# Attention and mixture of experts on one core: the softmax sums leave in two transfers instead of four

## The chip, the core and the metric

The kernel runs on one core of a Trainium2 chip. TensorE does the matmuls, VectorE and ScalarE work on tiles, GpSimd on tiles in SBUF, and the sync engine (SP) issues nearly all transfers. The metric is device time in microseconds, the median of several runs.

## The reference, cut to what matters

```python
q_rot, k_rot = (rotate(q), rotate(k))                 # batch 8, 8 heads, 576 positions, 64 wide
scores = scale * np.matmul(q_rot, k_rot.transpose(0, 1, 3, 2))
attn = np.exp(scores - np.max(scores, axis=-1, keepdims=True))
attn = attn / (np.sum(attn, axis=-1, keepdims=True) + 1e-09)
x = np.matmul(attn, v)                                # heads side by side: (4608, 512)
...
logits = x @ phi                                      # 32 slots, 4 for each of 8 experts
slot_input = softmax(logits, over tokens).T @ x
slot_out[e] = np.maximum(slot_input[e] @ w1[e], 0.0) @ w2[e]
return softmax(logits, over slots) @ slot_out
```

The change touches one thing: how the row sums of `exp(scores)` become factors 1/sum that are multiplied into the attention output.

## The kernel before, in words

Two heads make a pair; there are 32 pairs, four to a batch. A pair takes some 12.7 to 16 us, and the work of several pairs overlaps. The tables `WHEN`, `EARLY` and `ENDS` give each task of each pair a time, and the program is written out in the order of these times. So every engine, SP among them, has its instructions in a fixed order and waits in line at each.

The tasks of a pair, in the order in which they follow from each other: `load0` and `load1` fetch q and k (`x_in`, L171), `spin0` and `spin1` multiply by cosine and sine on GpSimd (L176), `join` adds on VectorE (L180), `high` and `low` split the result in two half-precision tiles (`hl`, L185 on ScalarE and L189 on VectorE). `m_unit` (L209, L211) makes the scores in one precision and takes their row maxima on VectorE; these go through `m_turn`, `m_half` and the two small transfers of `m_rows` (L239, L240) into a tile `peak`. `t_unit` (L257) makes the scores again, with the maxima subtracted by a matmul on `peak`, and ScalarE takes exp (L258). `av` (L273) multiplies by v. 

Then the sums, for the first 30 pairs. VectorE adds weight tables (`add1`, L287, and `add2`, L291). `total` (L304) sums over keys with matmuls by the selector `pick`; the sums lie in four blocks of 32 partitions (two halves n of the 576 positions, two partial sums k), and of each block two partitions count, one for each head. `total_out` (L309) copies them to `s4` on ScalarE. `send` (L315) re-cuts them by transfers from SBUF to SBUF: 2 partitions of 288 numbers become 48 partitions of `RC` = 12 numbers, four transfers in all. `recip` (L321, L322) adds the two partial sums and takes 1/x on VectorE. `spread` (L328) writes the result to a row in device memory (`r_row`), `widen` (L335) reads it back, repeated over 64 partitions for each head (`rb`), and `norm` (L339) multiplies on GpSimd. `logits` (L429) needs that product later.

On SP the order in a pair is: `x_in` (load0), a weight tile `w_exp`, `v_in`, the transfers of `send`, the two of `m_rows`, `x_in` (load1), `spread`, two of `widen`. Each transfer also waits for the one issued eight places ahead of it, because eight semaphores (DMAHW0 to DMAHW7) are given out in turn. On VectorE `recip` stands between `add1` and `add2`, and `low` comes right after.

The last two pairs take another way (`sums_rows`, `sums_turn`), which uses `pick` too. After the pairs come the experts: weights w1 and w2 stream in, and the output is written.

Of the kernel before, what the change touches and what calls it, by code (L numbers as in the profile page):

```python
# [7 lines left out]
F32 = mybir.dt.float32  # L8
# [3 lines left out]
ALU = mybir.AluOpType  # L12
AX = mybir.AxisListType
# [8 lines left out]
NS = E * SPE  # L22
# [4 lines left out]
HC = S // 2  # L27
# [16 lines left out]
N_HEAT = 16  # L44
N_CST = 2
FILL = (3, 1, 1, 2, 2, 5)
RC = 12
PIECE = 4
WHEN = {
# [40 lines left out]
def attn_softmoe(ctx, tc, qk, v, phi, w1, w2, cs, ident, sel, seg, out):  # L90
    nc = tc.nc
    P = 128

    const = ctx.enter_context(tc.tile_pool(name="const", bufs=1))
    small = ctx.enter_context(tc.tile_pool(name="small", bufs=3))
# [22 lines left out]
    rows = (slice(0, 64), slice(64, P))  # L118
# [11 lines left out]
    peaks = [const.tile([P, S], F16, name=f"peak{i}") for i in range(2)]  # L130
    for t in peaks:
        nc.vector.memset(t, 0.0)
    pick = const.tile([P, NS + 1], F32, name="pick")
    nc.gpsimd.memset(pick, 0.0)
    for h in (0, 1, 2):
        nc.gpsimd.memset(pick[rows[h % 2], h:h + 1], 1.0)

    nc.vector.memset(tiny, 0.0)
    for n in range(2):
        nc.vector.memset(tiny[64 * n:64 * n + 32], 1e-9)  # L140
    l_sb = const.tile([P, 2, 193], F32, name="l_sb")
    nc.vector.memset(l_sb[:, 0, 192:193], -BIG)
    d_t = const.tile([P, P], F32, name="d_t")
# [147 lines left out]
        nc.vector.tensor_tensor(out=c, in0=c, in1=weights_of(p, 4), op=ALU.add)  # L291

    sg = {}
    rcs = [const.tile([48, 2, 2, RC], F32, name=f"rc{i}") for i in range(2)]

    def total(p):
        c = cts.pop(p)
        sg[p] = s = bank2()[:, 0, 0:HC]
        for i in range(3):
            for n in range(2):  # L300
                for k in range(2):
                    at = 32 * (2 * n + k)
                    rhs = weights_of(p, 3 + 2 * i + k) if i else c[:, k]
                    nc.tensor.matmul(s[at:at + 32], lhsT=pick[:, n:n + NS], rhs=rhs[:, half[n]],  # L304
                                     start=(i == 0), stop=(i == 2), tile_position=(0, at))

    def total_out(p):
# [3 lines left out]

    def send(p, eng):
        s4, rc = sg.pop(p), rcs[p % 2]
        for i in range(4):
            eng.dma_start(out=rc[:, i // 2, i % 2, :], in_=s4[32 * i:32 * i + 2])  # L315

    rbs = {}

    def recip(p):
        rr = small.tile([48, 2, RC], F32, name="rr", bufs=2)  # L320
        nc.vector.tensor_reduce(out=rr, in_=rcs[p % 2].rearrange("p n k x -> p n x k"), axis=AX.X, op=ALU.add)  # L321
        nc.vector.reciprocal(out=rr, in_=rr)  # L322
        sg[p] = rr

    def spread(p, eng):
        rr = sg.pop(p)
        rd = dram.tile([2, 2, HC], F32, name="r_row")
        eng.dma_start(out=rd.rearrange("n h (r x) -> (h r) n x", x=RC), in_=rr)  # L328
        sg[p] = rd

    def widen(p, eng):
# [32 lines left out]
    def sums_rows(p):  # L364
        z = cts.pop(p)[:, 0]
        t = flat.pop("h") if "h" in flat else bank2()
        for i in range(4):
            nc.tensor.matmul(t[32 * i:32 * i + 32, 0, 0:HC], lhsT=pick[:, i % 2:i % 2 + NS], rhs=z[:, half[i % 2]],
                             start=True, stop=True, tile_position=(0, 32 * i))
        sg[p] = s4 = late.tile([P, HC], F32, name="s4", bufs=1)  # L370
        nc.vector.tensor_copy(out=s4, in_=t[:, 0, 0:HC])

    def sums_turn(p, t=None):
        s4, t = sg.pop(p), bank2() if t is None else t
        rn = small.tile([P, 3, 2, 2], F32, name="rn", bufs=2)
        for j, c in enumerate(turns):
            nc.tensor.transpose(t[:, 0, P * j:P * j + P], s4[:, c:c + P], id_sb)
        v = t[:, 0, 0:3 * P].rearrange("p (j n r) -> p j n r", j=3, r=32)
        nc.vector.reciprocal(out=rn, in_=v[:, :, 0:2, 0:2])
        sg[p] = rn  # L380

    def sums_wide(p, t=None):
# [344 lines left out]
    p = NPAIR - 1  # L727
# [8 lines left out]
    t = bank2()  # L736
# [288 lines left out]
```

## Time and profile before

| | |
|---|---|
| three runs | 566.99, 568.9, 570.32 us; median 568.9 |
| the profiled execution | 567.57 us, of which the span shown is 565.8 us |
| TensorE busy | 523.2 us, 92% of the span |
| VectorE, ScalarE, GpSimd busy | 77%, 57%, 52% |
| share of the 16 transfer engines | 60.2% for the kernel's own queue |

The shares are means over stages: a start of some 45 us, a long even stretch of pairs to about 500 us, and the experts. What an engine waited for is read in the stretch. Times are us from the start of the span; an engine's idle time is put down to what ended it.

### The profile page before, as it was taken

What the parts mean: (1) busy time and instruction counts of PE and PEld (TensorE: products, weight loads), DVE (VectorE), ACT (ScalarE), POOL (GpSimd) and SP (SyncE); (2) the same over time, 40 slices, a digit from 0 to 9 for tenths busy, and PEclk for the clock granted to TensorE, in tenths of its full rate; (3) what the DMA queues carried; (4) which work ended last, traced back from release to release, by engine and by line L of the source; (5) the groups of instructions that cost most, each with busy time, mean ns of one, the idle gap of its engine ahead of it and who ended that gap; (6) DMA issues with size and microseconds to landing.
All of it is one profiled execution on the core that took longest, in us unless ns stands there. A gap on an engine that the chain in (4) does not pass through costs nothing.

```text
span 565.8 us, 23624 instructions
## 1 busy us (share of the span) xinstructions
PE 523.2 (92%) x10302; PEld 351.2 (62%) x10302; DVE 435.9 (77%) x644; ACT 325.2 (57%) x639; POOL 296.0 (52%) x331
## 2 busy tenths in 40 slices
PE   4599999999989999999999999998999999999991
PEld 2266666666766676676666666666767665744551
DVE  5898989888888898788888888988888955642252
ACT  2156656666656565766676566665766665326641
POOL 2958666667656585865674848666656111011100
PEclk9599999999999999999999999999999999999997
DMA  7434555555564555555555556546635245999999
GB/s 261 153 105 166 188 187 187 187 187 185 161 203 157 189 187 187 188 187 185 185 192 173 197 144 222 174 134 197 196 125 186 76 134 163 308 346 346 331 304 293
DMA packets 69815, 111.38 MB, mean 197 GB/s; under 512 B 14416, under 2 KB 49488, under 8 KB 69712
## 3 DMA queue, kind: packets, MB, share of 16 engines
q1 hardware_dynamic: 69698, 109.87, 60.2%
q8 instruction: 81, 1.33, 1.0%
q14 instruction: 22, 0.18, 0.1%
q10 hardware_dynamic: 14, 0.00, 0.0%
HBM read 99.93 MB, written 9.58 MB: 194 GB/s over the span
## 4 chain that ended last, share of the span: by engine, by line
PE 62%; DVE 13%; DMA 10%; ACT 5%; SPq 4%; issue 4%; POOL 2%; DVEq 0%; ACTq 0%; POOLq 0%
PE o_ps L273 16%; PE s_ps L257 16%; PE s_ps L304 7%; PE s_ps L209 5%; DMA x_in<-in_qk 4%; DVE nm L211 3%; DVE hl L189 3%; DMA rc<-s 3%; PE s_ps L400 3%; SPq L315 3%; PE s_ps L866 2%; DMA rb<-r_row 2%; DVE c_t L291 2%; PE t_ps L918 2%; PE s_ps L429 2%
## 5 line engine op out<-in xcount | busy, mean ns | idle before, releaser
L176 POOL TENSOR_TENSOR x_in<-x_in,cs_sb 128x288 f32<-128x288 f32 x248 | 227.9, 951 | 105.3 <-DMA x_in<-in_qk 103.4
L211 DVE TENSOR_REDUCE nm<-s_ps 128x2 f32<-128x576 f32 x256 | 182.9, 750 | 53.0 <-PE s_ps L209 52.2
L258 ACT ACTIVATE a_t<-s_ps 128x576 f32<-128x576 f32 x256 | 161.0, 649 | 83.8 <-PE s_ps L257 73.3
L257 PE MATMUL s_ps<-hl 64*64 64x288 f16 x3456 | 158.7, 285 | 5.2 <-ACT xn L414 4.6
L273 PE MATMUL o_ps<-a_t,v_in 64*64 64x288 f32 x2048 | 161.6, 405 | 0.7 <-ACT xt L281 0.3
L257 PEld LDWEIGHTS <-hl 64*64 64x64 f16 x3456 | 100.6, 106 | 42.0 <-issue 26.9
L209 PE MATMUL s_ps<-hl 64*64 64x288 f16 x1024 | 82.9, 294 | 9.8 <-DVE nm L211 9.1
L257 PE MATMUL s_ps<-peak,lift 64*64 64x288 f16 x1152 | 89.4, 283 | 0.7 <-DMA peak<-mr 0.7
L273 PEld LDWEIGHTS o_ps<-a_t,v_in 64*64 64x64 f32 x2048 | 71.8, 133 | 17.1 <-ACT xt L281 4.5
L339 POOL TENSOR_TENSOR xt<-xt,rb 128x576 f32<-128x576 f32 x29 | 45.4, 1564 | 70.0 <-DMA rb<-r_row 63.5
L209 PEld LDWEIGHTS <-hl 64*64 64x64 f16 x1024 | 42.4, 106 | 34.0 <-issue 19.3
L185 ACT CAST hl<-x_in 128x576 f16<-128x576 f32 (+1 forms) x66 | 42.7, 651 | 24.1 <-DVE x_in L180 24.1
L180 DVE TENSOR_TENSOR x_in<-x_in 128x1152 f32<-128x1152 f32 (+2 forms) x36 | 52.6, 1462 | 3.2 <-POOL x_in L176 2.7
L287 DVE TENSOR_TENSOR c_t<-a_t 128x1152 f32<-128x1152 f32 x32 | 49.3, 1541 | 0.0
L189 DVE TENSOR_TENSOR hl<-x_in,hl 128x1152 f16<-128x1152 f32 x32 | 44.4, 1387 | 0.9 <-ACT hl L185 0.9
L309 ACT ACTIVATE s<-s_ps,bits 128x288 f32<-128x288 f32 x30 | 15.0, 501 | 47.0 <-PE s_ps L304 25.9
L257 PEld LDWEIGHTS <-lift 64*64 64x64 f16 x1152 | 38.6, 107 | 1.9 <-issue 0.9
L304 PE MATMUL s_ps<-a_t,pick 128*32 128x288 f32 x360 | 34.4, 406 | 0.0
L281 ACT COPY xt<-o_ps 128x576 f32<-128x576 f32 x32 | 20.4, 638 | 17.1 <-PE o_ps L273 13.0
L219 DVE TENSOR_REDUCE nm<-s_ps 128x2 f32<-128x576 f32 x32 | 24.0, 751 | 1.5 <-PE s_ps L217 0.2
L304 PEld LDWEIGHTS s_ps<-a_t,pick 128*32 128x32 f32 x360 | 15.2, 110 | 13.5
L414 ACT COPY xn<-s_ps 128x512 f32<-128x512 f32 x31 | 16.8, 589 | 11.0 <-PE s_ps L400 10.9
(202 smaller groups left out, 566.1 us busy)
## 6 DMA issues: line engine op xcount, KB each, us to landing
x_in<-in_qk SPq DMA_DIRECT2D x62, 576.0 KB
w_exp<-in_w SPq DMA_DIRECT2D x57, 512.0 KB
v_in<-in_v SPq DMA_DIRECT2D x32, 576.0 KB
rb<-r_row SPq DMA_DIRECT2D x60, 144.0 KB
out<-w_exp SPq DMA_DIRECT2D x16, 512.0 KB
hl<-in_w SPq DMA_DIRECT2D x4, 512.0 KB
rc<-s SPq DMA_DIRECT2D x120, 2.2 KB
x_in<-in_qk SPq DMA_DIRECT2D x4, 288.0 KB
```

The source lines that it names most:

```text
L176: eng.tensor_tensor(out=x[:, :, c], in0=x[:, :, c], in1=cs_sb[:, :, c], op=ALU.mult)
L180: nc.vector.tensor_tensor(out=x[:, t, 0, c], in0=x[:, t, 0, c], in1=x[:, t, 1, c], op=ALU.add)
L185: nc.scalar.copy(out=halves[p][:, 1 + t, c], in_=loaded[p][:, t, 0, c])
L189: nc.vector.tensor_tensor(out=hl[:, 0:4:3], in0=x[:, :, 0], in1=hl[:, 1:3], op=ALU.subtract)
L209: nc.tensor.matmul(s[rows[c], h, 0:HC], lhsT=hl[rows[h], QH, at:at + D], rhs=hl[rows[h], KH, half[n]], start=True, stop=True)
L211: nc.vector.tensor_reduce(out=nms[p][:, n, j:8:4], in_=s[:, :, 0:HC], axis=AX.X, op=ALU.max, negate=True)
L257: nc.tensor.matmul(s[rows[h ^ n], n, 0:HC], lhsT=lhs, rhs=rhs, start=(i == 0), stop=(i == 3))
L258: nc.scalar.activation(out=weights_of(p, b).rearrange("p (n x) -> p n x", n=2), in_=s[:, :, 0:HC], func=AF.Exp, scale=SCALE)
L273: nc.tensor.matmul(o[rows[h], n, 0:HC], lhsT=vt[r, b, n], rhs=a[r, half[n]], start=(b == 0), stop=(b == KB - 1))
L287: nc.vector.tensor_tensor(out=cts[p], in0=ats[p, 0], in1=ats[p, 1], op=ALU.add)
L304: nc.tensor.matmul(s[at:at + 32], lhsT=pick[:, n:n + NS], rhs=rhs[:, half[n]], start=(i == 0), stop=(i == 2), tile_position=(0, at))
L339: eng.tensor_tensor(out=xts[p], in0=xts[p], in1=rbs.pop(p), op=ALU.mult)
```

## The change

The two heads of a block come to lie 16 partitions apart instead of side by side (`pick` has its ones in columns 0, 16 and 32), and the blocks are put in the order k, then n. So the four rows of one partial sum lie at partitions 64k, 64k+16, 64k+32 and 64k+48, and one transfer with a step of 16 partitions takes them all. They are cut into 64 partitions of 18 numbers. `send` issues two transfers instead of four, `recip` works on 64 x 18 instead of 48 x 24 numbers, and `spread` writes 64 runs of 18 numbers instead of 96 of 12. No other task is moved. The small selector and the constant 1e-9 follow the new places, and `sums_turn` reads every 16th column.

```diff
--- before.py
+++ after.py
@@ -44,7 +44,8 @@
 N_HEAT = 16
 N_CST = 2
 FILL = (3, 1, 1, 2, 2, 5)
-RC = 12
+RC = 18
+HS = 16
 PIECE = 4
 WHEN = {
     "load0": -15.8683, "spin0": -15.5208, "load1": -12.695, "spin1": -12.6886, "join": -9.8416, "high0": -9.7692,
@@ -130,14 +131,13 @@
     peaks = [const.tile([P, S], F16, name=f"peak{i}") for i in range(2)]
     for t in peaks:
         nc.vector.memset(t, 0.0)
-    pick = const.tile([P, NS + 1], F32, name="pick")
+    pick = const.tile([P, NS + HS], F32, name="pick")
     nc.gpsimd.memset(pick, 0.0)
     for h in (0, 1, 2):
-        nc.gpsimd.memset(pick[rows[h % 2], h:h + 1], 1.0)
+        nc.gpsimd.memset(pick[rows[h % 2], HS * h:HS * h + 1], 1.0)
 
     nc.vector.memset(tiny, 0.0)
-    for n in range(2):
-        nc.vector.memset(tiny[64 * n:64 * n + 32], 1e-9)
+    nc.vector.memset(tiny[0:64], 1e-9)
     l_sb = const.tile([P, 2, 193], F32, name="l_sb")
     nc.vector.memset(l_sb[:, 0, 192:193], -BIG)
     d_t = const.tile([P, P], F32, name="d_t")
@@ -291,7 +291,7 @@
         nc.vector.tensor_tensor(out=c, in0=c, in1=weights_of(p, 4), op=ALU.add)
 
     sg = {}
-    rcs = [const.tile([48, 2, 2, RC], F32, name=f"rc{i}") for i in range(2)]
+    rcs = [const.tile([64, 2, RC], F32, name=f"rc{i}") for i in range(2)]
 
     def total(p):
         c = cts.pop(p)
@@ -299,9 +299,9 @@
         for i in range(3):
             for n in range(2):
                 for k in range(2):
-                    at = 32 * (2 * n + k)
+                    at = 32 * (2 * k + n)
                     rhs = weights_of(p, 3 + 2 * i + k) if i else c[:, k]
-                    nc.tensor.matmul(s[at:at + 32], lhsT=pick[:, n:n + NS], rhs=rhs[:, half[n]],
+                    nc.tensor.matmul(s[at:at + 32], lhsT=pick[:, HS * n:HS * n + NS], rhs=rhs[:, half[n]],
                                      start=(i == 0), stop=(i == 2), tile_position=(0, at))
 
     def total_out(p):
@@ -311,21 +311,21 @@
 
     def send(p, eng):
         s4, rc = sg.pop(p), rcs[p % 2]
-        for i in range(4):
-            eng.dma_start(out=rc[:, i // 2, i % 2, :], in_=s4[32 * i:32 * i + 2])
+        for k in range(2):
+            eng.dma_start(out=rc[:, k], in_=s4[64 * k:64 * k + 64:HS])
 
     rbs = {}
 
     def recip(p):
-        rr = small.tile([48, 2, RC], F32, name="rr", bufs=2)
-        nc.vector.tensor_reduce(out=rr, in_=rcs[p % 2].rearrange("p n k x -> p n x k"), axis=AX.X, op=ALU.add)
+        rr = small.tile([64, RC], F32, name="rr", bufs=2)
+        nc.vector.tensor_reduce(out=rr, in_=rcs[p % 2].rearrange("p k x -> p x k"), axis=AX.X, op=ALU.add)
         nc.vector.reciprocal(out=rr, in_=rr)
         sg[p] = rr
 
     def spread(p, eng):
         rr = sg.pop(p)
         rd = dram.tile([2, 2, HC], F32, name="r_row")
-        eng.dma_start(out=rd.rearrange("n h (r x) -> (h r) n x", x=RC), in_=rr)
+        eng.dma_start(out=rd.rearrange("n h (r x) -> (n h r) x", x=RC), in_=rr)
         sg[p] = rd
 
     def widen(p, eng):
@@ -365,7 +365,7 @@
         z = cts.pop(p)[:, 0]
         t = flat.pop("h") if "h" in flat else bank2()
         for i in range(4):
-            nc.tensor.matmul(t[32 * i:32 * i + 32, 0, 0:HC], lhsT=pick[:, i % 2:i % 2 + NS], rhs=z[:, half[i % 2]],
+            nc.tensor.matmul(t[32 * i:32 * i + 32, 0, 0:HC], lhsT=pick[:, i % 2 * HS:i % 2 * HS + NS], rhs=z[:, half[i % 2]],
                              start=True, stop=True, tile_position=(0, 32 * i))
         sg[p] = s4 = late.tile([P, HC], F32, name="s4", bufs=1)
         nc.vector.tensor_copy(out=s4, in_=t[:, 0, 0:HC])
@@ -376,7 +376,7 @@
         for j, c in enumerate(turns):
             nc.tensor.transpose(t[:, 0, P * j:P * j + P], s4[:, c:c + P], id_sb)
         v = t[:, 0, 0:3 * P].rearrange("p (j n r) -> p j n r", j=3, r=32)
-        nc.vector.reciprocal(out=rn, in_=v[:, :, 0:2, 0:2])
+        nc.vector.reciprocal(out=rn, in_=v[:, :, 0:2, 0::HS])
         sg[p] = rn
 
     def sums_wide(p, t=None):
```

The first place is the sync engine's queue at pair 23 (counted from 0), from the load of v on. `rc_135` and `rc_134` are the tables that `send` fills, `s_8685` and `s_8638` are `s4`. In the brackets is what an instruction waits for. Before:

```order
L195 DMA v_in<-in_v 128x1152 [waits DMAHW3_49,PE_49]
L315 DMA rc_135<-s_8685 48x1x12 [waits DMAHW4_49,Activation_49]
L315 DMA rc_135<-s_8685 48x1x12 [waits DMAHW5_49]
L315 DMA rc_135<-s_8685 48x1x12
L315 DMA rc_135<-s_8685 48x1x12 [waits DMAHW7_49]
L239 DMA peak_108<-mr 2x4x128 [waits DMAHW0_49,Activation_49]
L240 DMA peak_108<-mr 2x1x64 [waits DMAHW1_49]
L171 DMA x_in<-in_qk 128x1152 [waits DMAHW2_49]
L328 DMA r_row<-rr 48x2x12 [waits DMAHW3_49,DVE_49]
L335 DMA rb<-r_row 64x2x288 [waits DMAHW4_49,DMAHW3_49,Pool_49]
```

Changed:

```order
L195 DMA v_in<-in_v 128x1152 [waits DMAHW5_49,PE_49]
L315 DMA rc_134<-s_8638 64x1x18 [waits DMAHW6_49,Activation_49]
L315 DMA rc_134<-s_8638 64x1x18 [waits DMAHW7_49]
L239 DMA peak_108<-mr 2x4x128 [waits Activation_49]
L240 DMA peak_108<-mr 2x1x64 [waits DMAHW1_49]
L171 DMA x_in<-in_qk 128x1152 [waits DMAHW2_49]
L328 DMA r_row<-rr 64x18 [waits DMAHW3_49,DVE_49]
L335 DMA rb<-r_row 64x2x288 [waits DMAHW4_49,DMAHW3_49,Pool_49]
```

Two rows are gone, and every later transfer stands two places nearer. Since semaphores go out in turn, the transfer that each one waits for is still eight places back, which is now further back in time.

The second place is VectorE at the same pair, from the last row maxima before `add1` to the first after `low`. Before:

```order
L211 TENSOR_REDUCE nm_8576<-s_ps 128x2 [waits PE_49] x2
L287 TENSOR_TENSOR c_t<-a_t 128x1152 [waits Activation_49]
L321 TENSOR_REDUCE rr<-rc_135 48x24 [waits DMAHW6_49,DMAHW7_49,DMAHW5_49,DMAHW4_49]
L322 RECIPROCAL rr<-rr 48x24 [waits DVE_49]
L291 TENSOR_TENSOR c_t<-c_t,a_t 128x576 [waits Activation_49]
L189 TENSOR_TENSOR hl<-x_in,hl 128x2x576 [waits Activation_49]
L211 TENSOR_REDUCE nm_8576<-s_ps 128x2 [waits PE_49]
```

Changed:

```order
L211 TENSOR_REDUCE nm_8529<-s_ps 128x2 [waits PE_49] x2
L287 TENSOR_TENSOR c_t<-a_t 128x1152 [waits Activation_49]
L321 TENSOR_REDUCE rr<-rc_134 64x18 [waits DMAHW7_49,DMAHW6_49,DMAHW5_49]
L322 RECIPROCAL rr<-rr 64x18 [waits DVE_49]
L291 TENSOR_TENSOR c_t<-c_t,a_t 128x576 [waits Activation_49]
L189 TENSOR_TENSOR hl<-x_in,hl 128x2x576 [waits Activation_49]
L211 TENSOR_REDUCE nm_8529<-s_ps 128x2 [waits PE_49]
```

The order is the same. `recip` works on other shapes and waits for three semaphores instead of four, two of them those of `send`.

## Rows read from the trace of the kernel before

**Rows 1.** By stretch: busy PE, PEld, DVE, ACT, POOL; granted clock, DMA share, GB/s.

```profile
0.00:45.00 45.00, 28.14 (x398) 17.30 (x402) 35.60 (x55) 14.60 (x26) 27.24 (x42) 0.85 0.53 177
45.00:500.00 455.00, 442.34 (x9385) 305.29 (x9376) 379.93 (x553) 284.00 (x558) 264.25 (x284) 1.00 0.56 181
500.00:566.00 66.00, 52.77 (x529) 28.65 (x529) 20.37 (x38) 26.59 (x55) 4.54 (x7) 0.94 1.00 321
```

**Rows 2.** TensorE's waits, 45 to 566: us in total, times, longest.

```profile
PE s_ps L209 <- DVE nm L211: 4.9, 8, 1.1
PE s_ps L257 <- ACT xn L414: 4.6, 14, 0.3
...
PE s_ps L257 <- DMA peak<-mr: 0.7, 1, 0.7
...
PE s_ps L429 <- POOL xt L339: 0.2, 1, 0.2
```

**Rows 3.** The chain that ended last: shares by line; two pieces (start, us).

```profile
by line: PE o_ps L273 16.3%; PE s_ps L257 15.9%; PE s_ps L304 6.8%; PE s_ps L209 4.8%; DMA x_in<-in_qk 3.9%; issue 3.7%; DVE nm L211 3.2%; DVE hl L189 3.0%; DMA rc<-s 2.9%; PE s_ps L400 2.9%; SPq L315 2.7%; PE s_ps L866 1.9%; DMA rb<-r_row 
...
185.14 3.30 DMA r_row<-rr
...
268.37 1.80 DMA rc<-s
```

**Rows 4.** TensorE's timeline: first and last of eight stalls, and one.

```profile
57.51 0.32 PE L209 MATMUL s_ps<-hl 64*64 64x288 f16 x4 [0.59 <-DVE nm L211]
...
388.06 0.48 PE L257 MATMUL s_ps<-peak,lift 64*64 64x288 f16 x4 [0.66 <-DMA peak<-mr]
...
391.10 0.32 PE L209 MATMUL s_ps<-hl 64*64 64x288 f16 x4 [0.85 <-DVE nm L211]
```

**Rows 5.** VectorE's timeline at pair 3: start, busy us.

```profile
94.13 1.80 DVE L287 TENSOR_TENSOR c_t<-a_t 128x1152 f32<-128x1152 f32 x1
95.85 0.19 DVE L321 TENSOR_REDUCE rr<-rc 48x24 f32<-48x48 f32 x1
...
96.30 0.90 DVE L291 TENSOR_TENSOR c_t<-c_t,a_t 128x576 f32<-128x576 f32 x1
97.12 1.35 DVE L189 TENSOR_TENSOR hl<-x_in,hl 128x1152 f16<-128x1152 f32 x1
```

**Rows 6.** VectorE's timeline at pair 23.

```profile
384.75 1.55 DVE L287 TENSOR_TENSOR c_t<-a_t 128x1152 f32<-128x1152 f32 x1
387.98 0.20 DVE L321 TENSOR_REDUCE rr<-rc 48x24 f32<-48x48 f32 x1 [1.68 <-DMA rc<-s]
```

**Rows 7.** The sync engine's queue at pair 23: start, time of issuing.

```profile
382.01 2.73 SPq L315 DMA_DIRECT2D rc<-s  x4
384.85 0.53 SPq L239 DMA_DIRECT2D peak<-mr  x1
...
386.00 0.65 SPq L171 DMA_DIRECT2D x_in<-in_qk  x1
```

**Rows 8.** Single lines: count, ns min/median/max, first and last start, shapes.

```profile
L315 SPq DMA_DIRECT2D rc<-s x120: 604/628/695, 49.9 to 471.5; - x120
...
L321 DVEq EVENT_SEMAPHORE  x60: 21/35/1347, 53.1 to 477.3; - x60
L321 DVE TENSOR_REDUCE rr<-rc x30: 183/188/198, 54.4 to 478.0; 48x24 f32<-48x48 f32 x30
...
L322 DVE RECIPROCAL rr<-rr x30: 295/295/296, 54.6 to 478.3; 48x24 f32<-48x24 f32 x30
...
L379 DVE RECIPROCAL rn<-s_ps x2: 232/232/233, 482.1 to 492.3; 128x12 f32<-128x12 f32 x2
```

**Rows 9.** GpSimd's timeline at pair 3.

```profile
91.29 5.30 POOL L176 TENSOR_TENSOR x_in<-x_in,cs_sb 128x288 f32<-128x288 f32 x4
```

**Rows 10.** The sum over two weight tables on VectorE, all pairs.

```profile
L287 DVE TENSOR_TENSOR c_t<-a_t x32: 1295/1356/1999, 38.7 to 482.2; 128x1152 f32<-128x1152 f32 x32
```

**Rows 11.** The sync engine's wait for the table in memory.

```profile
SPq L335 <- DMA r_row<-rr: 68.1, 30, 4.1
```

## The prediction

> **What bounds the kernel now.** I began with the busy time by stretch. From 45 to 500 us TensorE works 442.3 of 455 us at the full granted clock [rows 1]; so at most some 13 us can be won there, whatever is done to the transfers. The experts behind it (500 to 566 us) hold none of the changed tasks, and the first 45 us hold none either but a few memsets. Next I asked what TensorE waits for [rows 2]. In the stretch of pairs it waits 4.9 us in eight places for VectorE's row maxima (L209 behind L211), 0.7 us in one place for `peak` and 0.2 us for a product of `norm`. These three, 5.8 us together, are all that can hang on the sums. The 4.6 us behind ScalarE's copies (L414) belong to another task.
>
> The chain that ended last seems to say more: it gives 2.7% of the span to SP's issuing of `send` (15.3 us) and 2.9% to its landing (16.4 us) [rows 3]. But the chain goes back along whatever came last at each step, also through waits that cost TensorE nothing; [rows 2] is the better bound.
>
> The timeline shows where the eight stalls lie: the first at 57.51 us, the last at 391.10 us [rows 4], six of the others in pairs 1, 3, 7, 11, 15 and 19. In these pairs VectorE has little time left between `add1` and the next row maxima, and `recip` stands in between. Pair 3 shows how: `add1` runs 94.13 to 95.93 us, `recip` starts at 95.85 (the entries overlap a little), then come `add2` and `low`, all back to back [rows 5]. So the transfer was there in time; VectorE is late because it is full. Only pair 23 is different: `add1` ends at 386.30, and VectorE stands idle 1.68 us for `rc` [rows 6]. There TensorE loses 0.85 us behind the maxima and 0.66 us on `peak`, which SP issued behind the four transfers of `send` [rows 4, 7].
>
> **The change part by part.** SP: four issues take 2.73 us at pair 23, about 0.68 each [rows 7], of which 0.63 is the issue itself [rows 8]. Two less free 2 x 0.68 = 1.36 us of SP in each of 30 pairs. The two transfers of `m_rows` and the fetch of load1 go out that much earlier. The issue of a merged transfer is not in the trace; the nearest row is the old one at 0.63 us, I take it, and even at twice that SP would be no later than now.
>
> The landing of `rc`: the last of four starts 2.05 us after the first and lands 1.80 us on [rows 3], in all 3.85. With two it is 0.68 + 1.80 = 2.48, if a merged transfer lands as fast as a single one. It moves 4.5 KB instead of 2.2, and no such transfer is in the trace; the lower bound is 1.80 us, the upper one `spread`, 4.5 KB too but to device memory, at 3.30 us [rows 3], which would give 3.98 and so no gain. I take 1.80, since both ends of this transfer are in SBUF as before.
>
> Perfetto Trace Analysis of the Trainium skill (section DMA Optimizations) says that with idle transfer engines a split into smaller pieces may let the whole end sooner, which speaks against this merge. The trace has the engines 56% busy in the stretch [rows 1], and pieces that start 0.68 us apart; by the page the merge would win nothing at the landing, and the time would be that of the second rival below.
>
> What an earlier landing is worth: in all tight pairs but 23 nothing, since `add1` covers it (pair 3: the step behind it begins as `add1` ends). At pair 23 `rc` lands 1.37 us earlier, and 0.31 of the 1.68 us would be left. `peak` goes out 1.36 us earlier too. So I count both of TensorE's losses as gone: 0.85 + 0.66 = 1.5 us. What made this one landing late no row shows, so it may come elsewhere in another execution; 0 is the lower bound of this term.
>
> VectorE: the reciprocal took 295 ns for 24 numbers and 232 ns for 12 [rows 8], so 5.3 ns a number, and 18 take about 263: 32 ns less. The reduction of 48 numbers takes 188 ns; 36 are a few ns less. One wait of 35 ns falls away [rows 8], behind `add1` where it costs nothing. So some 38 ns a pair. It counts only where TensorE waits for VectorE, in eight places: 0.3 us. In the other pairs VectorE has slack, and it is nothing.
>
> GpSimd: here the change acts at a distance. `add1` takes 1.36 us in the median but up to 2.00 [rows 10], and in pair 3 it takes 1.80 just while GpSimd takes 5.30 us for the four multiplies of `spin0` [rows 5, 9]. These multiplies wait for load0, which SP issues behind `widen`; and `widen` waits for `spread` to be in memory, 68.1 us in 30 pairs, so 2.3 us each [rows 11]. In front of `spread` in the queues is the bulk fetch of load1, which now goes out 1.36 us earlier. So `spin0` may begin up to 1.36 us earlier, and overlap less of `add1` and `add2`, and more of `join`, which VectorE can afford. With pair 23's 0.85 and the 0.3 us counted, 4.9 - 0.85 - 0.3 = 3.8 us of stalls are left. The ends of this term are +3.8 (all go) and a loss (the rival below). The gap of one collision, 1.80 - 1.36 = 0.44 us, is the nearest row; I take one such place won net, 0.5 us.
>
> The rest is nothing. The selector is 48 columns wide instead of 33 and is set on GpSimd in the first microseconds; the matmuls of `total` keep shape and order; one memset on VectorE less at the start lies before the first input has landed. `sums_turn` reads every 16th column in two instructions of 232 ns [rows 8]; even at twice that it is 0.5 us, at 482 and 492 us. `spread` has fewer and longer runs, which lies behind a wait that only GpSimd's `norm` sees.
>
> **The sum.** 1.5 + 0.3 + 0.5 = 2.3 us. The profiled execution's own time is 567.57 us (span 565.8 and 1.8 around it), so 565.3. That execution lies 1.3 us below the median of the runs shown, 568.9; against it I predict 566.6 us.
>
> **The rivals.** First, *the sums were the brake in every tight pair*: all of the 5.8 us go, 563.1 us. For it: all eight stalls stand right behind `recip`, and each of them is shorter than the 1.36 us that SP gains. Against it: VectorE is busy, not waiting, in seven of them.
>
> Second, *hidden*: pair 23 was an accident and its like comes back, and GpSimd's shift does nothing, or the merged transfer lands as late as the old four. Then only VectorE's 0.3 us are left: 568.6 us. For it: one landing in thirty was waited for.
>
> Third, *slower*: the earlier `spin0` collides with `low` or with `add1` where it is now clear of it. `add1` can grow by 2.00 - 1.36 = 0.64 us [rows 10]; in eight places that is 5.1 us, less the 1.8 of the first two terms, +3.3: 572.2 us. It decides from some 0.6 us in each of eight places on (4.7 us in all, for 0.5% net). For it: the two engines do hold each other up [rows 5, 9]. Against it: several tight pairs collide already and can only trade. SBUF — State Buffer of the Trainium skill (section Who interferes with whom) has it that a VectorE instruction with two inputs in SBUF and a GpSimd one that reads SBUF shut each other out for a whole instruction, the later one waiting; by that rule an earlier `spin0` would win or lose by whole multiplies, which the 1.80 beside 1.36 us agrees with and does not settle.
>
> Fourth, *the chain at its word*: half of SP's 15.3 us is on the path, -7.6 us, 561.3 us. Against it: TensorE does not wait so long in all.
>
> **How the numbers follow.** A change of 0.5% (2.8 us) is about what a measurement of this kernel can tell from none; the three runs lie 3.3 us apart. Chances: the forecast with a gain of 1 to 3.4 us 0.46 (a quarter of it beyond 0.5%), the first rival 0.21, hidden 0.21, slower 0.08, the chain 0.04. So faster by more than 0.5%: 0.12 + 0.21 + 0.04 = 0.37; slower 0.08; within 0.5% 0.55. The forecast's own range is 565.5 to 567.9 us. The whole range reaches to the first rival below, and above to the hidden case with 1 us for the spread of the runs: 563.1 to 569.6 us.
>
> **What would show it.** In the profile after: two issues of `send` in about 1.36 us; the reciprocal of `recip` near 263 ns; no idle time of VectorE for `rc` over 0.5 us; TensorE's wait for L211 at 3 to 4 us instead of 4.9; the fetch of load1 1.36 us earlier behind the copy to `s4`. It is wrong if TensorE's waits in the stretch stay at 5.8 us or grow, if the merged transfer lands over 3 us after its issue, or if `add1` and `low` grow in the tight pairs. If time goes elsewhere than in TensorE's waits, the whole account is wrong.

## The result, and the profile after

The changed kernel takes 563.44 us (median of 5 runs, 562.69 to 565.34); the kernel before, run beside it, 568.17 us (median of 5, 566.99 to 570.32). The ratio is 0.9895, 95% interval 0.9865 to 0.9925: 4.7 us less. The prediction was 566.6 us, 2.3 us less. Repeated later it was 563.85 against 568.59 us, ratio 0.9931 (0.9905 to 0.9957). So the gain is 4.7 us by the medians of either comparison, and 6.0 and 3.9 us by the two ratios; it lies outside the forecast's own range of 1 to 3.4 us and inside the whole range. The profiled execution took 562.69 us with a span of 560.9; the one before 567.57 and 565.8.

First the stretches, with the columns of [rows 1]:

```profile
0.00:45.00 45.00, 28.29 (x419) 17.61 (x421) 36.35 (x55) 14.68 (x27) 27.31 (x42) 0.85 0.55 182
45.00:500.00 455.00, 445.39 (x9409) 306.70 (x9403) 377.49 (x557) 284.33 (x558) 267.07 (x284) 1.00 0.57 185
500.00:566.00 66.00, 47.95 (x490) 25.63 (x482) 19.05 (x32) 26.62 (x55) 3.53 (x5) 0.93 0.87 291
```

In the middle stretch TensorE is busy 445.39 us instead of 442.34, at the same full granted clock: 3 us of waiting are gone. Next, what TensorE of the changed kernel waits for (us in total, times, longest), against [rows 2]:

```profile
PE s_ps L257 <- ACT xn L414: 4.6, 14, 0.3
PE s_ps L209 <- DVE nm L211: 2.5, 6, 0.6
...
PE s_ps L432 <- issue: 0.4, 1, 0.4
```

The wait for VectorE's maxima is 2.5 us instead of 4.9, that for `peak` (0.7) is gone. ScalarE's 4.6 us have not moved. The chain that ended last, by engine and by line as the page gives it, against [rows 3]:

```profile
PE 76%; DVE 9%; DMA 4%; ACT 4%; issue 3%; POOL 1%; SPq 1%; DVEq 0%; ACTq 0%; POOLq 0%
PE o_ps L273 22%; PE s_ps L257 21%; PE s_ps L304 8%; PE s_ps L209 6%; PE s_ps L400 3%; DVE nm L211 3%; DVE hl L189 2%; DVE c_t L287 2%; PE t_ps L918 2%; PE s_ps L429 2%; ACT xn L414 2%; PE o_ps L890 1%; PE s_ps L217 1%; DMA w_exp<-in_w 1%; PE s_ps L480 1%
```

`rc` and L315, 5.6% of the span together before, are no longer among the fifteen lines that the page lists: up to 31.7 us left the chain, and TensorE won 3 of them. The rest of this section follows these back. VectorE and the sync engine's queue at pair 23, against [rows 6, 7]:

```profile
379.33 1.23 SPq L315 DMA_DIRECT2D rc<-s  x2
381.43 0.56 SPq L239 DMA_DIRECT2D peak<-mr  x1
...
382.60 0.40 SPq L171 DMA_DIRECT2D x_in<-in_qk  x1
```

```profile
382.07 1.44 DVE L287 TENSOR_TENSOR c_t<-a_t 128x1152 f32<-128x1152 f32 x1
383.43 0.18 DVE L321 TENSOR_REDUCE rr<-rc 64x18 f32<-64x36 f32 x1
383.64 0.26 DVE L322 RECIPROCAL rr<-rr 64x18 f32<-64x18 f32 x1
```

`recip` starts as `add1` ends; the 1.68 us of waiting for `rc` are gone. But look at the queue: the two issues end at 380.56, and `peak` goes out only at 381.43. The queue's own waits, 45 to 500 us, say why:

```profile
SPq L328 <- DVE rr L322: 65.4, 30, 5.5
SPq L335 <- DMA r_row<-rr: 59.1, 30, 3.7
SPq L239 <- ACT hl L185: 36.5, 26, 1.5
```

SP now arrives at `m_rows` ahead of ScalarE's `mr` and waits there in 26 pairs, 1.4 us each (the row names a copy into `hl`; the tile that L239 sends, and has to wait for, is `mr`). So of the time that SP saves only a part reaches the fetch of load1 behind it. Against the start of the pair's `m_turn` on TensorE (L230), that fetch goes out at 2.47 us before and at 1.78 us now, 0.69 us earlier (medians of 23 pairs, from the two timelines).

The wait for `r_row` fell from 68.1 [rows 11] to 59.1 us. The small pieces came out as worked out: two issues of 586 ns in the median, and the reciprocal in

```profile
L322 DVE RECIPROCAL rr<-rr x30: 257/258/259, 53.7 to 473.6; 64x18 f32<-64x18 f32 x30
```

Where in the span the 4.9 us arise is read from one instruction that every pair has, L230 of TensorE. Its second and its last start, in the changed kernel:

```profile
37.63 0.28 PE L230 MATMUL s_ps<-id_sb,nm 128*9 128x128 f32 x1
...
466.04 0.28 PE L230 MATMUL s_ps<-id_sb,nm 128*9 128x128 f32 x1
```

In the trace before they stand at 38.49 and 470.73. So 0.9 us arise ahead of the pairs, where little but a few memsets changed, and 3.8 in between (432.24 us before, 428.41 now). I call this distance the stretch of pairs.

### The profile page after: what moved, and what is told of

It reads as the page before. It is cut to its first block, busy times and chain, and to the rows that moved or that the text cites. A ratio compares the mean times of both kernels' runs of the same rounds, so it can differ in the third digit from the quotient of the medians.

```text
span 560.9 us, 23481 instructions
## 1 busy us (share of the span) xinstructions
PE 521.6 (93%) x10302; PEld 349.9 (62%) x10302; DVE 432.9 (77%) x643; ACT 325.6 (58%) x639; POOL 297.9 (53%) x331
## 4 chain that ended last, share of the span: by engine, by line
PE 76%; DVE 9%; DMA 4%; ACT 4%; issue 3%; POOL 1%; SPq 1%; DVEq 0%; ACTq 0%; POOLq 0%
PE o_ps L273 22%; PE s_ps L257 21%; PE s_ps L304 8%; PE s_ps L209 6%; PE s_ps L400 3%; DVE nm L211 3%; DVE hl L189 2%; DVE c_t L287 2%; PE t_ps L918 2%; PE s_ps L429 2%; ACT xn L414 2%; PE o_ps L890 1%; PE s_ps L217 1%; DMA w_exp<-in_w 1%; PE s_ps L480 1%
## 5 line engine op out<-in xcount | busy, mean ns | idle before, releaser
L211 DVE TENSOR_REDUCE nm<-s_ps 128x2 f32<-128x576 f32 x256 | 182.8, 750 | 54.0 <-PE s_ps L209 53.5
L209 PE MATMUL s_ps<-hl 64*64 64x288 f16 x1024 | 82.6, 295 | 7.2 <-DVE nm L211 6.5
L209 PEld LDWEIGHTS <-hl 64*64 64x64 f16 x1024 | 42.2, 106 | 32.0 <-issue 16.8
L287 DVE TENSOR_TENSOR c_t<-a_t 128x1152 f32<-128x1152 f32 x32 | 47.0, 1467 | 0.0
```

The lines of the kernel that those rows point to most:

```text
L209: nc.tensor.matmul(s[rows[c], h, 0:HC], lhsT=hl[rows[h], QH, at:at + D], rhs=hl[rows[h], KH, half[n]], start=True, stop=True)
L211: nc.vector.tensor_reduce(out=nms[p][:, n, j:8:4], in_=s[:, :, 0:HC], axis=AX.X, op=ALU.max, negate=True)
L287: nc.vector.tensor_tensor(out=cts[p], in0=ats[p, 0], in1=ats[p, 1], op=ALU.add)
```

## The experiments

All kernels were timed beside the kernel before on the same chip; the chips differ, so times of two runs are set side by side only where that is said or against the kernel before. A table at the end of the section counts VectorE's time in twelve of the kernels.

**Is it a property of the change?** Both kernels again, unedited.

> The kernel before, unchanged, in a second profile. The comparison of the two traces left three theories. Issues: SP is free 1.36 us earlier in each pair, so what follows it (peak, the fetch of load1, the landing of rc) is earlier, and TensorE's short stalls behind L211 fall from 4.9 to 2.5 us. Shapes: recip is some 50 ns shorter, and that alone opens the tight pairs. Chance: some 0.9 us of the 4.9 arise before 45 us, where nothing changed, and 1.5 us are one late landing of rc at pair 23. By the chance theory this second profile has a stretch before 45 us that differs from the first by up to 1 us, and no wait for rc of 1.68 us at pair 23; TensorE's waits for L211 come to some 4 us. By the two others the waits for L211 are again near 4.9 us in some eight places. The time is within 0.3% of the kernel before by all of them.

> The changed kernel, unchanged, in a second profile and on another chip. If the 4.7 us are a property of the change, it is 4.3 to 5.5 us under the kernel before again. If 0.9 us of the start and 1.5 us of pair 23 were chance, it is some 2.3 to 3.5 us under it. TensorE's waits for L211 stay near 2.5 us in some six places by either.

The kernel before: ratio 1.001 (0.9983 to 1.0038). The changed kernel: 0.9931, 4.7 us by the medians and 3.9 by the ratio. The start is chance: the second L230 of the changed kernel stands at 38.67 us this time, behind the 38.20 of the kernel before, and the stretch of pairs is 428.34, beside 428.41; that of the kernel before is 432.47, beside 432.24. So the pairs give 3.8 and 4.1 us. But pair 23 was not the accident that a single profile makes it look like. In the second profile of the kernel before, VectorE waits for `rc` in three pairs, 1, 4 and 23:

```profile
67.49 0.20 DVE L321 TENSOR_REDUCE rr<-rc 48x24 f32<-48x48 f32 x1 [1.02 <-DMA rc<-s]
...
110.65 0.20 DVE L321 TENSOR_REDUCE rr<-rc 48x24 f32<-48x48 f32 x1 [1.07 <-DMA rc<-s]
...
387.58 0.20 DVE L321 TENSOR_REDUCE rr<-rc 48x24 f32<-48x48 f32 x1 [0.86 <-DMA rc<-s]
```

**The number of issues, or the new layout?** The changed layout with four transfers, and the old layout with two of its four, so that half of the sums are left out (their part of `rc` is set once at the start, which is cut here):

```
         for k in range(2):
-            eng.dma_start(out=rc[:, k], in_=s4[64 * k:64 * k + 64:HS])
+            for n in range(2):
+                at = 64 * k + 32 * n
+                eng.dma_start(out=rc[32 * n:32 * n + 32, k], in_=s4[at:at + 32:HS])
```

> The changed kernel with its new layout (heads 16 partitions apart, 64 x 18 numbers, the short recip, the new form of spread), but the sums leave in four transfers of 32 x 18 again. Theory issues: all but some 0.3 us of the gain goes, so 0 to 1 us under the kernel before. Theory shapes (recip and spread make the gain): it stays 4 to 5 us under the kernel before. A mixture lies between, and the distance to the changed kernel on the same chip is the price of two more issues.

```
-        for i in range(4):
+        for i in range(2):
             eng.dma_start(out=rc[:, i // 2, i % 2, :], in_=s4[32 * i:32 * i + 2])
```

> The kernel before with its old layout (48 x 12 numbers, the old recip and spread), but only the first two of the four transfers of send; the second half of rc is set once, so half of the sums are left out. If the number of issues alone makes the gain, it is 4 to 5 us under the kernel before, as the changed kernel was. If the new shapes are needed, 0 to 2 us under it.

Four transfers in the new layout: 567.89 against 568.59 us, ratio 0.9993 (0.9975 to 1.0012). The gain is gone; the changed kernel on the same chip had 563.85. So the layout alone is worth 0.7 us by the medians, and 1.4 at most by the interval. Two issues in the old layout: 566.58 against 569.39 us, 0.9941 (0.9916 to 0.9965): 2.8 us by the medians, 60% of the gain, with the old `recip`. So the number of issues decides most of it; whether the layout adds to it once there are two issues is open.

The Trainium skill's page Perfetto Trace Analysis (section DMA Optimizations), which the prediction weighed, has it that a split may help where transfer engines idle. Here four pieces against two of the same bytes cost 4 us, with the engines 56% busy in the stretch of pairs: the measurement decides, and in this place it goes the other way.

**Which work behind the two issues has to be early?** The changed kernel with two more transfers that nobody reads, at four places of SP's order: directly behind `send` (32 x 18 numbers out of `s4`), or, from a constant (32 x 16 numbers), behind `m_rows` (6.56 in the table of times, as in the diff), behind load1 (7.32), or ahead of `send` behind the fetch of v (9.22).

```
+    def more(p, eng):
+        for k in range(2):
+            eng.dma_start(out=spare[p % 2][:, k], in_=id_sb[64 * k:64 * k + 64:HS])
...
+    "more": 6.56,
```

> The changed kernel with two more transfers of 32 x 18 numbers from s4 behind the two of send, to a tile that nobody reads. rc lands as early as in the changed kernel, while SP comes to peak, load1 and spread as late as in the kernel before. If the earlier landing of rc is what counts (theory issues, by recip), the time is that of the changed kernel, 4 to 5 us under the kernel before. If what follows on SP counts (peak, the fetch of load1 and through it GpSimd), it loses most of the gain and is where the four transfers of the run beside it are, 0 to 1 us under the kernel before. By theory shapes it stays 4 to 5 us under it.

> The changed kernel with two more transfers (32 x 16 numbers from a constant to a tile that nobody reads) behind the two of m_rows, so rc and peak go out as early as in the changed kernel, and the fetch of load1 and spread up to 1.2 us later. If the early fetch of load1 is what pays, the gain goes: 0 to 1 us under the kernel before. If the early landing of rc or peak is, it stays 4 to 5 us under it. If the mere number of transfers in a pair counts, the gain goes here and in the two runs beside it alike.

> The same two more transfers behind the fetch of load1, ahead of spread, where SP of the changed kernel waits 65.4 us in 30 pairs for recip, 2.2 each. If rc, peak or the fetch of load1 pay by being early, nothing is lost: 4 to 5 us under the kernel before. If spread itself, and with it the later fetches, has to be early, part of it goes. If the number of transfers counts, all goes: 0 to 1 us.

> The same two more transfers ahead of send, behind the fetch of v, where SP waits for the copy to s4 some 80 us in 28 pairs, 2.8 each. By the account that SP's time between that copy and spread is what counts, this is the free place: 4 to 5 us under the kernel before. If the number of transfers counts (a semaphore that comes round sooner, or a queue that is longer), the gain goes: 0 to 1 us.

Behind `send`: ratio 1.0018 (0.9996 to 1.0041), all of the gain gone. Behind `m_rows`: 1.0034 (1.0011 to 1.0057), gone and more. Behind load1: 0.9907 (0.9883 to 0.9932), all kept. Ahead of `send`: 0.9910 (0.9888 to 0.9932), all kept. So it is not the count of transfers, and not `rc` or `peak` by themselves: behind `m_rows` these two were as early as in the changed kernel. What divides the four is whether the fetch of load1 is early. With two more behind `m_rows` it goes out at 2.98 us (median), later than before; with two more behind load1 at 1.77. Both kernels ran on one chip: 570.62 and 563.63 us, so 1.2 us at load1's fetch, in each pair, cost 7.0 us. What follows load1 on SP is not told apart from it: behind load1 the two cost `spread` and `widen` nothing, while behind `m_rows` `widen` goes out 0.6 us later (7.58 against 7.00 us behind L230, medians of 24 pairs), and TensorE waits 2.0 us for `norm`'s product. What a late load1 does is seen there at pair 19, on GpSimd and VectorE:

```profile
333.69 3.06 POOL L176 TENSOR_TENSOR x_in<-x_in,cs_sb 128x288 f32<-128x288 f32 x4 [4.92 <-DMA x_in<-in_qk]
```

```profile
335.35 0.17 DVE L223 TENSOR_REDUCE nm<-nm 128x9 f32<-128x18 f32 x1
336.79 1.36 DVE L180 TENSOR_TENSOR x_in<-x_in 128x1152 f32<-128x1152 f32 x1 [1.27 <-POOL x_in L176]
338.06 0.75 DVE L211 TENSOR_REDUCE nm<-s_ps 128x2 f32<-128x576 f32 x1
```

GpSimd waits 4.92 us for load1, its four multiplies end at 336.75, and `join` waits 1.27 us for them while the next maxima stand behind it. In the changed kernel `join` does not wait at this pair. In the trace before the same wait is there, and I had passed over it (VectorE's waits, 45 to 500 us):

```profile
DVE x_in L180 <- POOL x_in L176: 1.6, 3, 0.9
```

The two more directly behind `send` also show that an early issue is no early landing. At pair 1:

```profile
62.63 1.23 SPq L316 DMA_DIRECT2D rc<-s  x2
```

```profile
67.42 0.18 DVE L324 TENSOR_REDUCE rr<-rc 64x18 f32<-64x36 f32 x1 [0.95 <-DMA rc<-s]
```

Both issues are over at 63.86, and VectorE waits for `rc` until 67.42, 3.6 us on. The bulk fetches of weights and of v stand ahead in the same queue, issued 3.4 us earlier here and 4.2 us earlier in the changed kernel. That these held it up is argued, not shown.

**How late may load1 be?** One more transfer behind `m_rows` instead of two; and, the other way, `m_rows` or `send` given to ScalarE, or load1 ahead of `m_rows`.

```
-        for k in range(2):
+        for k in range(1):
             eng.dma_start(out=spare[p % 2][:, k], in_=id_sb[64 * k:64 * k + 64:HS])
```

> The changed kernel with one more transfer behind those of m_rows instead of two. Against the start of the pair's m_turn on TensorE the fetch of load1 goes out at 1.78 us in the changed kernel, at 2.47 in the kernel before, and at 2.98 with two more (medians of 23 pairs); with one more it should be at 2.4. If the start of load1 sets the time, it is within 1.5 us of the kernel before. If the count of transfers behind peak or something else made the two so slow, it is still near the changed kernel, 3 to 5 us under the kernel before.

```
-        eng.dma_start(out=pk[0:65:64, 512:S], in_=mr[8:9])
+        nc.scalar.dma_start(out=pk[0:65:64, 512:S], in_=mr[8:9])
```

> The changed kernel with the second, small transfer of m_rows issued by ScalarE, so load1 goes out at 1.2 us instead of 1.78. If earlier is still better here, up to 2 us under the changed kernel, 5 to 7 us under the kernel before. If the optimum is passed, as with load1 ahead of peak (-0.2 us, and nothing won), or if 0.6 us of ScalarE a pair cost TensorE something, 1 to 4 us above the changed kernel.

```
-        "m_rows": lambda p: m_rows(p, nc.sync),
+        "m_rows": lambda p: m_rows(p, nc.scalar),
...
-        "send": slow(lambda p: send(p, nc.sync)),
+        "send": slow(lambda p: send(p, nc.scalar)),
...
-    "load1": -12.695,
+    "load1": -13.5,
```

> The changed kernel with the two transfers of m_rows issued by ScalarE, 1.1 us of issue that leave SP, and SP no longer waits for mr ahead of load1 (36.4 us in 26 pairs). By the account, up to 2 us under the changed kernel; with ScalarE as the price, 2 to 10 us above it.

> The kernel before, four transfers in send, with m_rows issued by ScalarE. SP comes to load1 1.1 us earlier although the sums still leave in four. If SP's time ahead of load1 is what the change bought, this buys nearly as much: 3 to 5 us under the kernel before. If fewer transfers of the sums are needed (rc's landing), 0 to 1 us. If ScalarE pays, it is slower, and the run beside it shows the price.

> The changed kernel with send's two transfers issued by ScalarE, so that SP has none of them left between the copy to s4 and the fetch of load1 (another 1.2 us, where it does not wait for mr). By the account that came out of the runs before (VectorE waits for rc, waits in join for GpSimd's products, and is held up by GpSimd, all because SP is late with load1) the time is at most 2 us under the changed kernel, since TensorE's waits for L211 there are 2.5 us in all. If ScalarE's 1.2 us a pair delay its copies for TensorE (L258, L414: 4.6 us of waits now), it is slower than the changed kernel by 2 to 10 us.

> The changed kernel with the fetch of load1 ahead of m_rows, directly behind send. load1 goes out some 2 us earlier, peak 0.4 us later and behind 576 KB in the queue, which at 181 GB/s is 3.3 us. If load1 early is worth more still, it is under the changed kernel by up to 2 us. If peak has no slack (in the kernel before TensorE waited 0.66 us for it at pair 23), TensorE waits for it in many pairs and it is slower than both kernels, by 3 us a pair at the worst.

One more: 567.3 against 570.67 us, ratio 0.9936 (0.9911 to 0.9961), while load1 goes out at 2.41 us, nearly as late as in the kernel before. By the medians 3.4 us are left, 70% of the gain: the second expectation is met and the first is not. So the start of load1 does not set the time alone; here `rc` is early as well (its issues are those of the changed kernel). The profile, with a stretch of pairs of 432.36 us and 5.5 us of TensorE's waits for L211, looks like the kernel before, but that one was profiled again on another chip, and on this one it takes 570.67 us. How the 3.4 us arise stays open. Half of `m_rows` on ScalarE: 563.91 against 570.67 us, 0.9871 (0.9833 to 0.9909), load1 at 1.21 us. That is the best ratio of all, but not a time below the changed kernel's 563.44 and 563.85 on other chips; whether it is faster is open.

The others are no better. All of `m_rows` on ScalarE: 568.11 us in the changed kernel, 0.9982 (0.9954 to 1.0011), with load1 at -0.28 us, and 570.69 us in the kernel before, 1.0038 (1.0015 to 1.0060), with load1 at 1.23. `send` on ScalarE: 566.67 against 568.48 us, 0.9947 (0.9923 to 0.9971), with load1 at 1.86: more than half of the gain lost by the medians. Load1 ahead of `m_rows`, at -0.19 us: 568.02 us, 0.9989 (0.9964 to 1.0015). In the first three ScalarE has two issues more in each pair, so they do not show what an earlier load1 is worth by itself. But the two kernels with `m_rows` on ScalarE, on one chip, are 2.6 us apart with load1 early in both: some of what two issues fewer give does not go by a late load1. VectorE waits 1.35 us for `rc` in the one with four issues, and not at all in the other. With load1 ahead of `m_rows` TensorE stalls in pairs that had no stall before: pair 9, on GpSimd, VectorE and TensorE:

```profile
183.55 5.21 POOL L176 TENSOR_TENSOR x_in<-x_in,cs_sb 128x288 f32<-128x288 f32 x4 [1.89 <-DMA x_in<-in_qk]
```

```profile
185.41 1.95 DVE L189 TENSOR_TENSOR hl<-x_in,hl 128x1152 f16<-128x1152 f32 x1
187.28 2.74 DVE L211 TENSOR_REDUCE nm<-s_ps 128x2 f32<-128x576 f32 x4
```

```profile
188.08 0.32 PE L209 MATMUL s_ps<-hl 64*64 64x288 f16 x4 [0.67 <-DVE nm L211]
```

GpSimd's multiplies of load1 now run beside `add1`, `add2` and all of `low`: four take 5.21 us instead of 3.06, `low` 1.95 instead of 1.35 us, and the maxima come late. The same stall stands at pairs 17, 21 and 25. This is like the prediction's third rival, with load1's multiplies in place of `spin0`, and met when load1 is moved 2 us and not 0.7. It is not all of the loss: TensorE's waits for L211 are 3.4 us against 2.5, those for `peak` 1.3 us, and the stretch of pairs is 4.3 us longer than in the changed kernel.

**By which way does a late load1 cost time?** I took VectorE's two waits away by its order: `recip` behind `add2`, `join` one maximum later.

```
-    "recip": 7.3881,
+    "recip": 7.46,
...
-    "join": -9.8416,
+    "join": -9.81,
```

> The kernel before with recip behind add2 on VectorE instead of ahead of it: rc may land 0.7 us later without being waited for, while SP comes to load1 as late as ever. In the profiles of four-issue kernels VectorE waited 1.7 to 3.0 us for rc, in one to three pairs. If the landing of rc is a term of its own, 1 to 2 us under the kernel before. If it is worth nothing without the early load1 (as with the two transfers behind peak, where rc was early and nothing was won), within 0.5 us of it.

> The kernel before with join one row maximum later on VectorE in most pairs, so that it waits less for GpSimd's products of load1, with load1 as late as ever. VectorE waited 1.6 us for them in three places. If that wait is the way by which load1 counts, 1 to 2 us under the kernel before. If load1 counts by the overlap of GpSimd with VectorE (elongated add1, low, join), join only moves and may collide more: within 1 us of it, or slower.

> The kernel before with recip behind add2 and join one maximum later. If the gain of the change is VectorE's two waits (for rc and for GpSimd's products), the kernel with four transfers gets most of it: 3 to 4 us under the kernel before, near the changed kernel. If it is the timing of GpSimd against VectorE, 0 to 1 us.

> The changed kernel with recip behind add2. Its profiles had one wait for rc of 0.3 to 0.5 us, in a pair where TensorE loses nothing, so by every theory it is within 1 us of the changed kernel, 4 to 5 us under the kernel before; under it if rare late landings that the profiles did not catch cost it something.

These told little of what they were made for. `recip` later: 1.0006 (0.9980 to 1.0032) in the kernel before, 0.9980 (0.9954 to 1.0006) in the changed one, where it loses 3 us or more. A reason is in the row of `add2`, in the changed kernel with `recip` later:

```profile
L291 DVE TENSOR_TENSOR c_t<-c_t,a_t x30: 741/826/1229, 43.2 to 458.4; 128x576 f32<-128x576 f32 x30
```

It takes 826 ns in the median where it took 686 in both kernels: directly behind `add1`, whose table it reads and writes, it is slower than with `recip` between them. From the end of `add1` to the start of `low` it is 1.58 us instead of 0.92 (medians of the 15 pairs in which nothing else stands between them), with the same four instructions. Later `spread` may add to it. `join` one maximum later costs 24 us (1.0399, 1.0343 to 1.0454; with `recip` later 1.0413, 1.0370 to 1.0457), since ScalarE's copies of its result stand ahead of `mr` (TensorE's waits in the kernel before with `join` later):

```profile
PE s_ps L257 <- ACT mr L234: 18.4, 17, 1.3
```

So `join` may not be late. That a wait for load1 in front of it is dear for the same reason is likely, but not shown.

**The sum over the tight pairs.** What the kernels' traces do give is a count of VectorE's time, in one execution of each. For the eight stretches from one L230 to the next in which `recip` of pairs 0, 1, 3, 7, 11, 15, 19 and 23 runs I added up, from the timelines, its waits for `rc`, its waits for GpSimd, the busy time of `join`, `add1`, `add2` and `low`, and that of `recip`, in us. Beside it stand TensorE's wait for L211 at L209 (45 to 500 us), the stretch of pairs, and the median start of load1 after L230:

```
kernel                        rc  GpSimd   sums  recip   total | L209  stretch  load1
before                      1.68    1.63  44.09   3.87   51.27 |  4.9   432.24   2.47
before, again               1.88    1.63  44.02   3.88   51.41 |  5.9   432.47   2.47
four transfers, new layout  2.42    1.27  44.65   3.47   51.81 |  5.8   433.53   2.47
two more behind send        2.36    1.29  43.90   3.47   51.02 |  4.9   432.94   2.47
two more behind m_rows      0.27    2.74  45.41   3.47   51.89 |  4.3   432.78   2.98
one more behind m_rows      0.66    1.57  45.94   3.45   51.62 |  5.5   432.36   2.41
changed                     0       0.85  42.98   3.45   47.28 |  2.5   428.41   1.78
changed, again              0       1.17  43.47   3.44   48.08 |  3.0   428.34   1.78
old layout, two of four     0       1.08  43.73   3.83   48.64 |  1.8   430.62   1.74
two more behind load1       0       0.87  42.37   3.46   46.70 |  1.7   428.87   1.77
two more ahead of send      0       0.38  43.14   3.45   46.97 |  2.2   427.69   1.79
half of m_rows on ScalarE   0       0.71  42.94   3.45   47.10 |  2.3   430.17   1.21
```

The totals fall into two groups, 51.0 to 51.9 and 46.7 to 48.6, and the start of load1 parts them; the kernel with one more behind `m_rows` stands in the first group by its trace and nearer to the second by its ratio. The stretch of pairs follows roughly: with the old layout and with half of `m_rows` on ScalarE TensorE waited besides for `norm`'s product, 0.9 and 2.0 us, and with two more behind `m_rows` 2.0 us as well. It does not follow in the kernels left out: `send` on ScalarE has 48.5 with a stretch of 431.97 us, `m_rows` on ScalarE 48.0 with 434.81 (changed) and 49.0 with 435.13 (before), load1 ahead of `m_rows` 50.6 with 432.71. Between the first row and that of the changed kernel lie 4.0 us: 1.7 for `rc`, 0.8 for GpSimd's products, 1.1 of shorter additions, 0.4 of `recip`. Between the two repeats lie 3.3 us: 1.88, 0.46, 0.55 and 0.44 in the same order. The terms trade with each other: with two more behind `m_rows`, `rc` is nearly free, and the products and the additions take it all back.

## Why the prediction was right in direction and half in size

- **Where the time went.** In TensorE's waits behind VectorE's maxima and on `peak`, as predicted: 2.4 and 0.7 us in the profiled pair of executions, 2.9 and none in the repeats. 0.9 us of the 4.9 arose ahead of the pairs and were chance, as the repeats show; the prediction's rule that time elsewhere would make the account wrong is met to that extent. The rest of the 3.8 and 4.1 us of the pairs, some 0.5 and 1.2 us, is not traced.
- **Pair 23, 1.5 us.** Nearly right in size: of TensorE's 0.85 us 0.30 are left, and the 0.66 on `peak` are gone, so 1.2 us; in the repeats 1.48 us became 0.50, and there was no wait on `peak`. It is better founded than I knew. The four profiles with four issues and `m_rows` on SP (the kernel before twice, four transfers in the new layout, two more behind `send`) all have it, with 1.68, 0.86, 0.70 and 1.41 us; VectorE waited for `rc` in one to three pairs of each, 1.7 to 3.0 us in all. My sentence that in all tight pairs but 23 an earlier landing is worth nothing was read from one execution: in the three others pair 1 had the wait too. With `m_rows` on ScalarE in the kernel before, pairs 0 and 1 had it and pair 23 did not.
- **`recip`, 0.3 us.** Right: 258 ns where 263 were worked out, and 0.4 us over eight tight pairs.
- **GpSimd, 0.5 us. This is the step that failed**, the term of the sum that was mis-sized. In the seven tight pairs other than 23 TensorE's waits for L211 fell from 4.0 to 2.2 us, and in the repeats from 4.4 to 2.5: 1.8 and 1.9 us, where this term and that of `recip` had 0.8 together. The count of VectorE's time gives 1.9 us to GpSimd in the first pair of traces (0.8 of waits that fell away, 1.1 of additions that became shorter) and 1.0 in the repeats. And the two unread transfers put ahead of load1 instead of behind it cost 7.0 us. I had load1 earlier and GpSimd's work with it, but followed it through `spin0` behind `spread` and `widen`, and held that `join` is something "which VectorE can afford". A nearer way is load1's own multiplies and `join`'s wait for them; that wait stood in the trace before with 1.6 us in three tight pairs, and `join` later in every pair costs 24 us. Spin0 moved too: `widen` goes out 0.2 us earlier, and the fetch of load0 0.25. How much goes by which way is argued from the count, not shown.
- **SP, 1.36 us earlier.** Wrong by half: `m_rows` now waits for `mr`, and load1 gains 0.69 us. A wait further on in the same queue took up the rest. Whether that made the gain smaller is open: load1 2 us earlier, ahead of `m_rows`, collided with `low`, but with half of `m_rows` on ScalarE load1 went out 0.6 us earlier and nothing was lost.
- **The landing, 1.80 us behind its issue.** Not a property of the transfer. The 1.80 us are read at 268 us; at pair 23, which the prediction worked out with them, the chain of the kernel before has twice as much:

```profile
384.14 3.71 DMA rc<-s
```

And the prediction's sign of being wrong, a merged transfer that lands over 3 us after its issue, is there in the changed kernel at pair 12, on SP and on VectorE:

```profile
218.70 1.25 SPq L315 DMA_DIRECT2D rc<-s  x2
```

```profile
224.60 0.18 DVE L321 TENSOR_REDUCE rr<-rc 64x18 f32<-64x36 f32 x1 [0.50 <-DMA rc<-s]
```

The issues are over at 219.95, and VectorE waits until 224.60, 4.7 us on. TensorE lost nothing by it there.

- **The rivals.** The first comes nearest in time, 563.1 against 563.44 us, but not in its mechanism: 2.5 us of stalls are left, and VectorE is still full in the tight pairs. The second, a gain of 0.3 us, is excluded by both intervals. The third is real, but sets in further out. SBUF — State Buffer of the Trainium skill (section Who interferes with whom) speaks of whole instructions that shut each other out; here `low` beside GpSimd grew by 0.60 us while GpSimd's four multiplies grew by 2.15, which agrees with mutual blocking (the 2.15 fell beside `add1`, `add2` and `low` together). The fourth, the chain at its word, promised 7.6 us and is too large.

## What to carry to other kernels

Fewer issues on a queue pay by what stands behind them in it: walk down the queue to the next wait, count how much of the gain survives it, and price the work that is released there, not the transfer that was merged. Where an engine is full, sum its waits and its lengthened instructions over the tight places and over two profiles; one landing that was waited for in one execution is a sample of a margin, not an accident. Small waits of such an engine for a slow neighbour (here 1.6 us in three places) belong in that sum, before any guess about how the two overlap.

## What was not expected of the hardware

- `add2` directly behind `add1`, in place on the same table, took 826 ns in the median, and 686 ns with `recip` between: so of the 0.43 us of `recip` between them about a third costs nothing.
- One transfer of 64 x 18 numbers took 586 ns to issue in the median, one of 48 x 12 took 628; here twice the bytes cost the queue no more.
- `spread` in its new form, one run of 18 numbers on 64 partitions, took 522 ns to issue in the median instead of 332, with the same bytes. SP's wait behind it, for `r_row`, still fell by 9 us in 30 pairs.
